# Windowed attention and a softplus feed-forward on one core: q, k and v in rotating buffers, x transposed by DMA from block 6

## The chip, the cores and the metric

The kernel runs on one core of a Trainium2 chip. The metric is the device time of one launch in microseconds. The kernel before takes 225.42 us (median of three runs, 224.99 to 226.09).

## What is computed

Attention over 4 batches, 8 heads, 768 positions and a head size of 64, then a two-layer feed-forward with softplus. Each query sees its own and the 95 positions before it, and the first 8 positions of its batch; a bias falls with the distance, with a slope for each head.

```python
B, H, S, D = 4, 8, 768, 64           # n_global 8, n_local 96
scores = q @ k.T / sqrt(D) - slopes * dist
a = softmax(where(is_global | is_local, scores, -1e9))
x = (a @ v).transpose(0, 2, 1, 3).reshape(3072, 512)
h = x @ w_in                         # w_in 512 x 2048
out = (max(h, 0) + log1p(exp(-abs(h)))) @ w_out   # w_out 2048 x 512, out 3072 x 512
```

All arrays are float32 in memory; the kernel multiplies in bfloat16 and sums in float32.

## The kernel before

The 3072 tokens are cut into 24 blocks of 128 (6 of them a batch) and 12 chunks of 256. Attention goes by blocks, the feed-forward by chunks. The program is a list of named steps, and the order in which they are recorded is the order in which each engine executes its share. The steps for block n:

- `t`: TensorE transposes q and k of the block (4 matmuls each), VectorE copies them to `QT` and `KT`. From block 8 (`NDT`) on it is `d` instead: two transposing DMAs on the SyncE queue (SP), lines 226 and 227.
- `gk`, `gv`: VectorE copies the 8 global rows of the batch's first block into `KT` and `v_t` of the block before.
- `s`: scores of half the heads, 8 matmuls into `s_ps` (line 253), and VectorE adds the bias (`Z`, line 260).
- `e`: ScalarE's exponential (`Pb`, line 266).
- `p`: 8 matmuls of `Pb` with `v_t` into `x_ps` (line 279). A column of ones at the end of each head of `v_t` gives the sum of weights; VectorE divides by it (`xsf`, lines 290 and 293).
- `x`: transposes `xsf` into half of a chunk's `XT`, by TensorE (line 308) and a VectorE copy (line 311) below block 12 (`NDX`), by a transposing DMA on SP from there on (line 304).

The feed-forward has 8 steps `f` a chunk (f0 to f95): 8 matmuls of `w_in` with the chunk's `XT` (line 324), then ScalarE's exponential and logarithm (lines 329, 330). Chunk c reads `XT` of blocks 2c and 2c+1, so f24 to f31 read blocks 6 and 7. It has 8 steps `o` (o0 to o95): 4 matmuls of 512 columns (line 338); after each fourth VectorE copies the sum (`osb`, line 344) and SP stores it (line 346).

`opening()` does blocks 0 and 1 with filler matmuls (`warm`, line 384). Then comes a list written by hand, `ORDER`, up to about f23. All later steps are sorted by due times in units of one `f` (`steady(n)`; `f{u}` at u + 0.5, `o{u}` at u + 13.9).

Loads are issued by GpSimd, cast from float32 to bfloat16 by the DMA: 128 KB as written for each of q, k and v of a block, 512 KB for each quarter of `w_in` and `w_out`. The program before has a buffer of its own for each of the 24 blocks of q, k and v; all loads stand in the GpSimd queue from the start, in the order blocks 1 to 3 with `w_in`, blocks 4 and 5, `w_out`, blocks 6 to 23. A load waits for the landing of the eighth load before it, so at most eight are under way. [...]

Of the kernel before, what the change touches and what calls it, by code (L numbers as in the profile page):

```python
# [12 lines left out]
BF16 = mybir.dt.bfloat16  # L13
# [6 lines left out]
def kernel(  # L20
# [12 lines left out]
    P = nc.NUM_PARTITIONS  # L33

    B, H, S, D = q.shape
# [16 lines left out]
    NWC = 4  # L52
# [7 lines left out]
    const = ctx.enter_context(tc.tile_pool(name="const", bufs=1))  # L60
# [7 lines left out]

    NB = 2 * NCH
    BPB = 2 * CPB  # L70
    q_t = [const.tile([P, H, D], BF16, name=f"q_t{n}") for n in range(NB)]
    k_t = [const.tile([P, H, D], BF16, name=f"k_t{n}") for n in range(NB)]
    v_t = [const.tile([P, H, D + 1], BF16, name=f"v_t{n}") for n in range(NB)]
    w_in_c = [const.tile([P, KM, FW], BF16, name=f"w_in{c}") for c in range(NWC)]
    w_out_c = [const.tile([P, NFB // NWC, DM], BF16, name=f"w_out{c}") for c in range(NWC)]

# [5 lines left out]
    def ones(lo, hi):  # L82
        for n in range(lo, hi):
            nc.vector.memset(v_t[n][:, :, D : D + 1], 1.0)  # L84
# [5 lines left out]
    def load(n, src, dst):  # L90
        b, i = divmod(n, BPB)
        nc.gpsimd.dma_start(  # L92
            dst[n][:, :, 0:D], src[b, :, i * P : (i + 1) * P, :].rearrange("h s d -> s h d")
        )

    def load_w_in(c):
        nc.gpsimd.dma_start(  # L97
            w_in_c[c][:],
            moe_w_in[:, c * FW : (c + 1) * FW].rearrange("(m p) f -> p m f", p=P),
        )  # L100

    def load_w_out(c):
        nc.gpsimd.dma_start(  # L103
            w_out_c[c][:],
            moe_w_out[c * FW : (c + 1) * FW, :].rearrange("(a p) c -> p a c", p=P),
        )

    def load_block(n):
        load(n, q, q_t)
        load(n, k, k_t)  # L110
        load(n, v, v_t)

    _tables = list(get_activation_tables(nc.m.arch).keys())
    nc.scalar.add_instruction(
        mybir.InstLoadActFuncSet(
            name=nc.get_next_instruction_name(),
# [30 lines left out]
    def tables():  # L147
        nc.vector.tensor_scalar(
            far_a[:], rampf[:], float(NL - 1), FAR, op0=ALU.is_gt, op1=ALU.mult
        )  # L150
        nc.vector.tensor_scalar(far_b[:], rampf[:], 0.0, FAR, op0=ALU.is_lt, op1=ALU.mult)
        nc.vector.tensor_tensor(far_a[:], far_a[:], far_b[:], ALU.add)
        nc.vector.tensor_tensor(dist_d[:], far_a[:], rampf[:], ALU.add)
        nc.vector.tensor_copy(dist_0[:], dist_d[:])
        nc.vector.tensor_scalar_min(dist_0[0:NG, :], dist_0[0:NG, :], float(NL))
        nc.vector.tensor_scalar(
            far_b[:], rampf[:], -float(P - NL + 1), FAR, op0=ALU.is_gt, op1=ALU.mult
        )
        nc.vector.scalar_tensor_tensor(dist_p[:], rampf[:], float(P), far_b[:], ALU.add, ALU.add)
        nc.vector.memset(dist_p[0:NG, :], float(NL))  # L160

    tables()
    ones(2, NB)

    load_block(2)
    load_block(3)
    load_w_in(2)
    load_w_in(3)
    load_block(4)
    load_block(5)  # L170
    for c in range(NWC):
        load_w_out(c)
    for n in range(6, NB):
        load_block(n)

    def head_of(half, r):
        return 4 * half + 2 * ((r // 2) % 2) + r // 4
# [1 line left out]
    def bias_first(half):  # L179
        for r in range(0, 8, 2):  # L180
            nc.scalar.mul(bias0[:, half, r // 2, :], dist_0[:], -slopes[head_of(half, r)])

    def bias_rest(half):
        for r in range(8):
            nc.scalar.mul(
                biasA[:, half, r, :], (dist_p if r % 2 else dist_d)[:], -slopes[head_of(half, r)]
            )
# [27 lines left out]
        copy(KT[n][:], tr[:, 1, :, :])  # L215

    NDT = 8
    NDX = 12

    def dma_qk(n):  # L220

# [23 lines left out]
    def sc(n, half):  # L245

        first = n == first_of(n)
        for t in range(1 if first else 2):
            for mm in range(2):
                for sub in range(2):  # L250
                    m = 2 * half + mm
                    rows = slice(64 * sub, 64 * sub + 64)
                    nc.tensor.matmul(  # L253
                        s_ps[:, 4 * sub + 2 * mm + t, :], KT[n - t][rows, m, :], QT[n][rows, m, :]
                    )
        Z = work.tile([P, 8, P], F32, tag="Z", name="Z")
        if first:
            nc.vector.tensor_tensor(Z[:, 0:4, :], s_ps[:, 0:8:2, :], bias0[:, half, :, :], ALU.add)  # L258
        else:
            nc.vector.tensor_tensor(Z[:], s_ps[:], biasA[:, half, :, :], ALU.add)  # L260
        Zt[n, half] = Z

    def ex(n, half):
        nreg = 4 if n == first_of(n) else 8
        Pb = work.tile([P, 8, P], BF16, tag="Pb", name="Pb")
        nc.scalar.activation(  # L266
            Pb[:, 0:nreg, :], Zt.pop((n, half))[:, 0:nreg, :], AF.Exp, scale=inv_sqrt
        )
        Pt[n, half] = Pb
# [28 lines left out]
    def tr_x(n):  # L298
        xsf, _ = xt.pop(n)
        if n % 2 == 0:  # L300
            XT[n // 2] = xtp.tile([P, NPAIR, CT], BF16, tag="XT", name="XT")
        dst = XT[n // 2][:, :, P * (n % 2) : P * (n % 2) + P]
        if n >= NDX:
            nc.sync.dma_start_transpose(dst, xsf[:].rearrange("p h d -> p (h d)"))
            return
        tr = ps.tile([P, 2, NPAIR, P], BF16, tag="tr", name="tr")
        for m in range(NPAIR):
            nc.tensor.transpose(  # L308
                tr[:, 0, m, :], xsf[:, 2 * m : 2 * m + 2, :].rearrange("p a b -> p (a b)"), ident[:]
            )  # L310
        nc.vector.tensor_copy(dst, tr[:, 0, :, :])  # L311
# [20 lines left out]
    def ffn2(c, u):  # L332
# [14 lines left out]


    LAG = 13
    KINDS = {"t": tr_qk, "d": dma_qk, "gk": gk, "gv": gv, "s": sc, "e": ex, "p": pv, "x": tr_x}  # L350

    ORDER = """
        gk2 f0 gv2 t2 f1 s2.0 e2.0 f2 t3 s2.1 e2.1 gk3 f3 p2.0 s3.0 e3.0 f4 p2.1 gv3 s3.1
        e3.1 gk4 f5 x2 p3.0 f6 t4 p3.1 f7 x3 s4.0 f8 f9 s4.1 f10 f11 e4.0 e4.1 t5 o0 o4 gk5 f12
        gv4 p4.0 f13 s5.0 e5.0 o1 p4.1 o2 s5.1 gv5 f14 x4 o3 p5.0 t6 o5 e5.1 p5.1 f15 s6.0 x5 o6
        e6.0 s6.1 e6.1 t7 d8 p6.0 f16 f17 p6.1 s7.0 e7.0 o8 x6 f18 s7.1 gk8 e7.1 d9 o9 p7.0 f19
        f20 p7.1 gv8 s8.0 e8.0 d10 f21 o7 x7 s8.1 e8.1 gk9 f22 p8.0 f23
    """  # L360

    def steady(n):

        s = 4 * n - 13
        return {
            f"d{n}": s - 5.6, f"gk{n}": s - 0.85, f"s{n}.0": s + 0.1, f"e{n}.0": s + 1.2,
            f"s{n}.1": s + 2.1, f"e{n}.1": s + 3.2, f"gv{n}": s + 3.15, f"p{n}.0": s + 3.7,
            f"p{n}.1": s + 5.2, f"x{n}": s + (6.3 if n < NDX else 5.8),
        }

    def run(name):
# [4 lines left out]
        else:  # L376
            KINDS[kind](*nums)

    warm_ps = ps2.tile([P, DM], F32, tag="hT", name="warm_ps")

    def warm(count):

        for _ in range(count):
            nc.tensor.matmul(warm_ps[:], warm_in[:, 0:P], warm_in[:])  # L384

    def tr_first_q(n):
        tr = qk_bank()
        tr_in(tr, 0, q_t[n])
        to_QT(n, tr)

    def tr_first_k(n):
        tr = ps2.tile([P, 2, NPAIR, P], BF16, tag="o", name="tr_k")
        tr_in(tr, 1, k_t[n])
        to_KT(n, tr, nc.vector.tensor_copy if n == 0 else nc.scalar.copy)

    def opening():

        warm(8)
        bias_first(0)
        bias_first(1)  # L400
        bias_rest(0)
        bias_rest(1)
        nc.vector.tensor_copy(q_t[0][:], q_f[:])
        nc.vector.tensor_copy(k_t[0][:], k_f[:])
        tr_first_q(0)
        warm(1)
        tr_first_k(0)
        warm(2)
        sc(0, 0)
        ex(0, 0)  # L410
        tr_first_q(1)
        tr_first_k(1)
        warm(1)
        sc(0, 1)
        ex(0, 1)
        warm(1)
        pv(0, 0)
        sc(1, 0)
        ex(1, 0)
        warm(1)  # L420
        pv(0, 1)
        warm(2)
        sc(1, 1)
        tr_x(0)
        ex(1, 1)
        warm(3)
        pv(1, 0)
        warm(5)
        pv(1, 1)
        warm(3)  # L430
        tr_x(1)
        warm(1)

    opening()
    first_steps = ORDER.split()
    for name in first_steps:
        run(name)
    todo = {}
    for n in range(NDT, NB):
        todo.update(steady(n))  # L440
    for u in range(NU * NCH):
        todo[f"f{u}"] = u + 0.5
        todo[f"o{u}"] = u + LAG + 0.9
# [37 lines left out]
```

## Time and profile before

| | before |
|---|---|
| median of three runs | 225.42 us (224.99 to 226.09) |
| the profiled execution | 224.88 us |
| its span, first to last instruction | 223.1 us |
| granted TensorE clock | 0.997 |
| TensorE busy | 212.8 us (95%) |
| ScalarE busy | 162.6 us (73%) |
| VectorE busy | 116.4 us (52%) |
| GpSimd busy, nearly all in issuing loads | 68.4 us (31%) |
| loads of q, k and v | 70, median 9.4 to 9.5 us from issue to landing |
| transposing DMAs | 44 (16 of q, 16 of k, 12 of x) |

The page of the profile gives busy times of the engines (PE is TensorE, PEld its weight loads, DVE VectorE, ACT ScalarE, POOL GpSimd, SP SyncE), a row of digits for 40 equal slices of the span, the chain of work that ended last, followed back from the end, and the costliest groups of instructions by line. In answers of the trace, the arrow `out<-in` names the tiles written and read, and a bracket gives the engine's idle time before an instruction and what ended it. An engine that is not the bound may sit idle at no cost.

### The profile page before, as it was taken

The page shows a single profiled execution, that of the slowest core. Times are in us where ns is not written, and L with a number is a line of the kernel's source. Part 1 is how long each engine was busy: PE and PEld are TensorE (multiplying, and loading weights), DVE is VectorE, ACT ScalarE, POOL GpSimd, SP SyncE. Part 2 cuts the span into 40 slices and gives each one's busy share as a digit, 9 for nine tenths or more (in the row PEclk, how much of TensorE's full clock was granted, in tenths as well). Part 3 has the DMA queues.
Part 4 walks back from the last instruction along what each step waited for, and adds up shares of the span by engine and source line. Part 5 has one row for each costly group of instructions (what it writes and reads, how often), then busy time and mean ns, then how long its engine had stood idle before and what let it go on. Part 6 is the DMA issues. An engine that isn't in the chain of part 4 may idle for free.

```text
span 223.1 us, 4879 instructions
## 1 busy us (share of the span) xinstructions
PE 212.8 (95%) x1964; PEld 140.2 (63%) x1996; DVE 116.4 (52%) x263; ACT 162.6 (73%) x266; POOL 68.4 (31%) x85
## 2 busy tenths in 40 slices
PE   7889999999899999999999999999999999999993
PEld 2457776677667676667666666666666666666541
DVE  7767864866775565464464563454654653011121
ACT  7738999669698768768878878688788787677200
POOL 8958563696668568550000000000000000000000
PEclk9999999999999999999999999999999999999998
DMA  9999999999999999999912622721433220111112
GB/s 129 164 173 191 167 200 203 158 183 127 150 182 175 156 180 181 130 182 181 156 51 69 119 60 62 121 81 40 118 86 35 72 73 18 53 50 47 47 51 90
DMA packets 106518, 26.27 MB, mean 118 GB/s; under 512 B 99328, under 2 KB 103424, under 8 KB 106496
## 3 DMA queue, kind: packets, MB, share of 16 engines
q0 software_dynamic: 77024, 13.37, 77.4%
q1 hardware_dynamic: 29472, 12.59, 28.3%
q8 instruction: 15, 0.25, 0.4%
q14 instruction: 7, 0.06, 0.1%
HBM read 27.26 MB, written 6.29 MB: 150 GB/s over the span
## 4 chain that ended last, share of the span: by engine, by line
PE 72%; DMA 22%; POOL 3%; issue 1%; DVE 0%; POOLq 0%
PE o L338 33%; PE hT L324 31%; DMA w_in<-in_moe_w_in_dram 9%; DMA w_out<-in_moe_w_out_dram 6%; PE s_ps L253 5%; DMA KT<-k_t 3%; PE x_ps L279 3%; DMA k_t<-in_k_dram 3%; POOL v_t L92 1%; PE tr L308 1%; POOL w_out L103 1%; POOL q_t L92 0%; POOL k_t L92 0%; POOL w_in L97 0%; DVE osb L344 0%
## 5 line engine op out<-in xcount | busy, mean ns | idle before, releaser
L324 PE MATMUL hT<-XT,w_in 128*128 128x256 bf16 x768 | 99.2, 273 | 1.2 <-DVE XT L311 0.7
L338 PE MATMUL o<-w_out,G 128*128 128x512 bf16 x354 | 91.0, 379 | 1.6
L329 ACT ACTIVATE e_sb<-hT 128x512 f32<-128x512 f32 x96 | 56.5, 588 | 35.9 <-PE hT L324 35.7
L324 PEld LDWEIGHTS <-w_in 128*128 128x128 bf16 x768 | 70.6, 98 | 18.2 <-issue 0.7
L330 ACT ACTIVATE G<-e_sb 128x512 bf16<-128x512 f32 x96 | 60.5, 630 | 3.1
L260 DVE TENSOR_TENSOR Z<-s_ps,biasA 128x1024 f32<-128x1024 f32 x40 | 48.8, 1220 | 12.1 <-PE s_ps L253 10.2
L338 PEld LDWEIGHTS <-G 128*128 128x128 bf16 x384 | 36.0, 98 | 27.7
L266 ACT ACTIVATE Pb<-Z 128x1024 bf16<-128x1024 f32 (+1 forms) x48 | 46.6, 973 | 5.4 <-DVE Z L260 4.4
L344 DVE COPY osb<-o 128x512 f32<-128x512 f32 x24 | 16.6, 692 | 44.5 <-PE o L338 44.5
L290 DVE RECIPROCAL rcp<-x_ps 128x4 f32<-128x4 f32 x48 | 8.7, 181 | 37.2 <-PE x_ps L279 37.2
L92 POOL DMA_DIRECT2D v_t<-in_v_dram x24 | 21.3, 888 | 10.8 <-DMA q_t<-in_q_dram 3.9
L92 POOL DMA_DIRECT2D k_t<-in_k_dram x23 | 20.5, 891 | 7.6 <-DMA v_t<-in_v_dram 4.3
L92 POOL DMA_DIRECT2D q_t<-in_q_dram x23 | 20.6, 896 | 4.7 <-DMA k_t<-in_k_dram 2.8
L253 PEld LDWEIGHTS <-KT 64*128 64x128 bf16 x352 | 10.2, 94 | 18.6 <-issue 15.4
L293 DVE TENSOR_TENSOR xsf<-x_ps,rcp 128x256 bf16<-128x256 f32 x48 | 20.4, 424 | 1.7
L279 PEld LDWEIGHTS <-Pb 128*128 128x128 bf16 x352 | 16.8, 98 | 6.6 <-ACT Pb L266 1.1
L253 PE MATMUL s_ps<-QT,KT 64*128 64x128 bf16 x352 | 18.2, 219 | 2.0 <-DMA KT<-k_t 0.9
L279 PE MATMUL x_ps<-v_t,Pb 128*128 128x65 bf16 x352 | 18.6, 193 | 0.4 <-ACT Pb L266 0.3
L384 PE MATMUL warm_ps<-warm_in 128*128 128x512 bf16 x26 | 9.5, 485 | 1.2 <-DVE v_t L84 1.2
L258 DVE TENSOR_TENSOR Z<-s_ps,bias 128x512 f32<-128x512 f32 x8 | 5.5, 690 | 2.8 <-PE s_ps L253 2.6
L243 DVE COPY v_t<-v_t 8x512 bf16<-8x512 bf16 x16 | 5.6, 353 | 0.0
L311 DVE COPY XT<-tr 128x512 bf16<-128x512 bf16 x12 | 5.0, 415 | 0.8 <-PE tr L308 0.8
(39 smaller groups left out, 51.9 us busy)
## 6 DMA issues: line engine op xcount, KB each, us to landing
out_dram<-osb SPq DMA_DIRECT2D x24, 256.0 KB, 2.2
v_t<-in_v_dram POOLq DMA_DIRECT2D x24, 128.0 KB, 9.4
q_t<-in_q_dram POOLq DMA_DIRECT2D x23, 128.0 KB, 9.4
k_t<-in_k_dram POOLq DMA_DIRECT2D x23, 128.0 KB, 9.5
w_in<-in_moe_w_in_dram POOLq DMA_DIRECT2D x4, 512.0 KB, 9.5
w_out<-in_moe_w_out_dram POOLq DMA_DIRECT2D x4, 512.0 KB, 11.8
q_f<-in_q_dram SPq DMA_DIRECT2D x1, 256.0 KB, 3.2
k_f<-in_k_dram SPq DMA_DIRECT2D x1, 256.0 KB, 3.8
```

What stands on the lines that cost most here:

```text
L92: nc.gpsimd.dma_start(dst[n][:, :, 0:D], src[b, :, i * P : (i + 1) * P, :].rearrange("h s d -> s h d"))
L253: nc.tensor.matmul(s_ps[:, 4 * sub + 2 * mm + t, :], KT[n - t][rows, m, :], QT[n][rows, m, :])
L260: nc.vector.tensor_tensor(Z[:], s_ps[:], biasA[:, half, :, :], ALU.add)
L266: nc.scalar.activation(Pb[:, 0:nreg, :], Zt.pop((n, half))[:, 0:nreg, :], AF.Exp, scale=inv_sqrt)
L279: nc.tensor.matmul(x_ps[:, lh, :], Pb[:, r, :], v_t[n - t][:, h, :], start=(t == 0), stop=(t == 1 or first),)
L293: nc.vector.tensor_tensor(xsf[:, h0 : h0 + 4, :], x_ps[:, :, 0:D], rcp[:, h0 : h0 + 4][:, :, None].to_broadcast([P, 4, D]), ALU.mult,)
L324: nc.tensor.matmul(hT[:, j, :], w_in_c[wc][:, m, fo : fo + P], XT[c][:, m, :], start=(m == 0), stop=(m == KM - 1),)
L329: nc.scalar.activation(e_sb[:], hT[:], AF.Exp)
L330: nc.scalar.activation(G[c][:, 2 * u : 2 * u + 2, :], e_sb[:], AF.Ln, bias=1.0)
L338: nc.tensor.matmul(o[:], G[c][:, 4 * kq + a, ns * P : ns * P + P], w_out_c[kq][:, a, :], start=(kq == 0 and a == 0), stop=(kq == NWC - 1 a ...
L344: nc.vector.tensor_copy(osb[:], O.pop((c, ns))[:])
L384: nc.tensor.matmul(warm_ps[:], warm_in[:, 0:P], warm_in[:])
```

## The change

q and k get four buffers each and v eight, shared by the blocks in rotation. The loads of blocks 6 and 7 and later become steps of their own, `l` (q and k) and `lv` (v), in `ORDER` and, from block 8, by due times. A load into a buffer in rotation waits until the block that had it has been read: q and k of block n+4 until q and k of block n are transposed, v of block n+8 until the last reader of v of block n. The column of ones is set eight times instead of 24. `NDX` goes from 12 to 6, so x of blocks 6 to 11 is transposed by DMA on SP. `ORDER` is replaced and reaches f26.

In the new order as built, SP's queue has, between the transposes of blocks 8 and 13: q8, k8, q9, k9, the output of o7, x6, q10, k10, the output of o11, x7, q11, k11, q12, k12, x8, x9.

```diff
-    q_t = [const.tile([P, H, D], BF16, name=f"q_t{n}") for n in range(NB)]
-    k_t = [const.tile([P, H, D], BF16, name=f"k_t{n}") for n in range(NB)]
-    v_t = [const.tile([P, H, D + 1], BF16, name=f"v_t{n}") for n in range(NB)]
+    RQK = 4
+    RV = 8
+    q_r = [const.tile([P, H, D], BF16, name=f"q_t{n}") for n in range(RQK)]
+    k_r = [const.tile([P, H, D], BF16, name=f"k_t{n}") for n in range(RQK)]
+    v_r = [const.tile([P, H, D + 1], BF16, name=f"v_t{n}") for n in range(RV)]
+    q_t = [q_r[n % RQK] for n in range(NB)]
+    k_t = [k_r[n % RQK] for n in range(NB)]
+    v_t = [v_r[n % RV] for n in range(NB)]
...
-    def load_block(n):
+    def load_qk(n):
         load(n, q, q_t)
         load(n, k, k_t)
+
+    def load_v(n):
         load(n, v, v_t)
...
     tables()
-    ones(2, NB)
+    ones(2, RV)
...
-    load_block(4)
-    load_block(5)
-    for c in range(NWC):
-        load_w_out(c)
-    for n in range(6, NB):
-        load_block(n)
...
-    NDX = 12
+    NDX = 6
...
-    KINDS = {"t": tr_qk, "d": dma_qk, "gk": gk, "gv": gv, "s": sc, "e": ex, "p": pv, "x": tr_x}
+    KINDS = {
+        "t": tr_qk, "d": dma_qk, "gk": gk, "gv": gv, "s": sc, "e": ex, "p": pv, "x": tr_x,
+        "l": load_qk, "lv": load_v,
+    }
...
-        gk2 f0 gv2 t2 f1 s2.0 e2.0 f2 t3 s2.1 e2.1 gk3 f3 p2.0 s3.0 e3.0 f4 p2.1 gv3 s3.1
-        e3.1 gk4 f5 x2 p3.0 f6 t4 p3.1 f7 x3 s4.0 f8 f9 s4.1 f10 f11 e4.0 e4.1 t5 o0 o4 gk5 f12
-        gv4 p4.0 f13 s5.0 e5.0 o1 p4.1 o2 s5.1 gv5 f14 x4 o3 p5.0 t6 o5 e5.1 p5.1 f15 s6.0 x5 o6
-        e6.0 s6.1 e6.1 t7 d8 p6.0 f16 f17 p6.1 s7.0 e7.0 o8 x6 f18 s7.1 gk8 e7.1 d9 o9 p7.0 f19
-        f20 p7.1 gv8 s8.0 e8.0 d10 f21 o7 x7 s8.1 e8.1 gk9 f22 p8.0 f23
+        f0 t2 l6 lv6 gk2 gv2 f1 s2.0 e2.0 f2 t3 l7 lv7 s2.1 gk3 e2.1 f3 p2.0 s3.0 e3.0 f4 p2.1
+        gv3 s3.1 e3.1 gk4 f5 x2 p3.0 f6 t4 l8 p3.1 f7 gv4 x3 s4.0 f8 f9 e4.0 s4.1 f10 e4.1 t5 l9
+        f11 gk5 o0 f12 s5.0 p4.0 o4 e5.0 f13 o1 p4.1 gv5 lv8 s5.1 e5.1 o5 o2 p5.0 x4 f14 p5.1 t6
+        l10 o3 f15 lv9 s6.0 x5 e6.0 o6 s6.1 e6.1 t7 l11 d8 p6.0 f16 f17 d9 s7.0 e7.0 p6.1 o7 f18
+        s7.1 o8 o9 e7.1 p7.0 o10 x6 gk8 d10 f19 lv10 p7.1 gv8 f20 l12 s8.0 e8.0 f21 o11 s8.1 o12
+        gk9 p8.0 e8.1 f22 lv11 s9.0 f23 p8.1 e9.0 x7 o13 gv9 s9.1 o14 e9.1 f24 l13 gk10 p9.0 f25
+        s10.0 f26 lv12 d11 d12 p9.1
...
-            f"p{n}.1": s + 5.2, f"x{n}": s + (6.3 if n < NDX else 5.8),
+            f"p{n}.1": s + 5.2, f"x{n}": s + 5.8,
...
     opening()
+    load_block(4)
+    load_block(5)
+    for c in range(NWC):
+        load_w_out(c)
...
+    for n in range(RV, NB):
+        todo[f"l{n}"] = 4 * n - 27
+        todo[f"lv{n}"] = 4 * n - 21.5
```

More of the change, by code (lines that the diff above doesn't have):

```diff
@@ L106, in load_w_out, with load_block @@
         )
-    def load_block(n):
+    def load_qk(n):
         load(n, q, q_t)
         load(n, k, k_t)
+    def load_v(n):
         load(n, v, v_t)
+    def load_block(n):
+        load_qk(n)
+        load_v(n)
     _tables = list(get_activation_tables(nc.m.arch).keys())
```

## The prediction

> **What bounds the kernel now.** I read the page first, then the chain of waits, then the timeline of TensorE (PE), then the landing times of the transposing DMAs in two stretches. From the page, busy time, the DMA row of the 40 slices, and the chain's shares:
>
> ```profile
> PE 212.8 (95%) x1964; PEld 140.2 (63%) x1996; DVE 116.4 (52%) x263; ACT 162.6 (73%) x266; POOL 68.4 (31%) x85
> ...
> DMA  9999999999999999999912622721433220111112
> ...
> PE 72%; DMA 22%; POOL 3%; issue 1%; DVE 0%; POOLq 0%
> ```
>
> PE sets the time; the 22% of DMA in the chain lies early, and the DMA engines are full for the first 20 slices (to about 108 us) and nearly empty later. Where DMA enters the chain last:
>
> ```profile
> 41.85 7.24 DMA k_t<-in_k_dram
> 49.11 7.60 DMA KT<-k_t
> 56.76 0.40 PE s_ps L253 x8
> ```
>
> k of block 8 lands, is transposed by DMA in 7.6 us, and PE waits for it. In the table of PE's waits none is later than this one. The timeline of PE around it (start, duration, idle before in brackets):
>
> ```profile
> 53.69 1.91 PE L324 MATMUL hT<-XT,w_in 128*128 128x256 bf16 x16
> 55.43 0.41 PE L279 MATMUL x_ps<-v_t,Pb 128*128 128x65 bf16 x8
> 56.76 0.40 PE L253 MATMUL s_ps<-QT,KT 64*128 64x128 bf16 x8 [0.92 <-DMA KT<-k_t]
> ...
> 62.78 0.41 PE L279 MATMUL x_ps<-v_t,Pb 128*128 128x65 bf16 x8
> 63.03 1.04 PE L324 MATMUL hT<-XT,w_in 128*128 128x256 bf16 x8
> 63.90 1.03 PE L338 MATMUL o<-w_out,G 128*128 128x512 bf16 x4
> 64.86 0.40 PE L253 MATMUL s_ps<-QT,KT 64*128 64x128 bf16 x8
> 65.19 0.40 PE L308 MATMUL tr<-ident,xsf 128*128 128x128 bf16 x4
> 65.42 1.04 PE L324 MATMUL hT<-XT,w_in 128*128 128x256 bf16 x8
> 66.30 1.03 PE L338 MATMUL o<-w_out,G 128*128 128x512 bf16 x4
> 67.16 1.04 PE L324 MATMUL hT<-XT,w_in 128*128 128x256 bf16 x8
> ```
>
> Matmuls overlap, so a step's price is the distance of starts: f 0.87 (63.03 to 63.90), o 0.86 (66.30 to 67.16), s 0.33 (64.86 to 65.19), p 0.25 (62.78 to 63.03), a PE transposition of x 0.23 (65.19 to 65.42). Last, the DMA transposes of k, from issue to landing, first while loads fill the queues (57 to 106 us), then after them (106 us on):
>
> ```profile
> L227 SPq DMA_TRANSPOSE KT<-k_t x6: 1282/1344/1675, 56.6 to 101.2; - x6
> DMA to landing us min/median/max: 7.0/7.6/8.2
> ...
> L227 SPq DMA_TRANSPOSE KT<-k_t x8: 1195/1216/1220, 109.4 to 167.1; - x8
> DMA to landing us min/median/max: 2.4/2.4/3.9
> ```
>
> The same transfer takes 2.4 us alone and 7.6 us beside the loads. This pair of rows decides the case.
>
> **The change, part by part.** *x by DMA from block 6.* x6 to x11 leave PE: 6 x 0.23 = 1.4 us, all on the path, as PE is the bound where they stand (51 to 91 us). Their 6 VectorE copies (0.42 us each) were beside PE's work: nothing. *Memsets.* Sixteen fewer of the v ones (17 take 0.64 us in VectorE's timeline): nothing, because the cast of k behind them sits idle 0.46 us for its own DMA. *Loads.* Their number and prices stay (0.88 us of GpSimd each). Each now also waits until its rotating buffer is read; behind a waiting load stand only later loads. Load n is due 4n-27, its DMA transpose 4n-18.6: 8.4 steps of f, and a block of four takes 8.3 us (starts 105.0 to 113.3 us), so 17 us, against 9.5 us that a load takes in full queues. Nothing. Up to k of block 8 the sequence of loads is what it was, so 49.1 us stays the landing of k8 and about 56.7 us that of its transpose.
>
> *The order.* Ahead of f20 now stand two more o steps (o7, o10) and p7.1, and no x6: 0.86 + 0.86 + 0.25 - 0.23 = 1.7 us. So f20, at 54.56 before (0.87 behind the row of 53.69), starts at 56.3, and the scores of block 8 behind it at 57.1, after their KT has landed: the 0.92 us of waiting is covered. If that transpose took 8.2 us, 0.2 us of it would come back.
>
> *The new wait.* f24 needs x7 transposed. On PE it was made at 58.8 and f24 started at 63.0 without a wait. Now x7 is a DMA on SP, behind the output of o11, which waits for VectorE's copy of o11. PE reaches the end of o11 after f20, s8.0, f21, o11: 56.3 + 0.87 + 0.33 + 0.87 + 0.86 = 59.2, 0.2 more until its results are out; copy 0.69 (osb group of the page), output issue 0.33 and pauses 0.2: x7 is issued at about 60.6. PE is ready for f24 after s8.1, o12, p8.0, f22, s9.0, f23, p8.1, o13, s9.1, o14 more: 3 x 0.33 + 3 x 0.86 + 2 x 0.25 + 2 x 0.87 = 5.8, so at 59.2 + 5.8 = 65.0. x7 has 4.4 us. The landing is bounded by the rows above: 2.4 us (no wait) and 8.2 us (wait 3.8); 8.5 is the longest for q (3.9 ... 4.1). Which is nearer? By 60.6 us the load sequence has run as before through v of block 10; q12 and k12 then wait for the transposes of q8 and k8 (about 55 and 57 us) and v11, q13, k13 follow at GpSimd's 0.9 us, so some five loads stand in the queues where before there were eight, but SP has three transposes and two outputs of its own in flight. I take 7.2 us, a little under the median of the full queues: x7 lands at 67.8, f24 waits 2.8 us. Nothing hides this: f24 to f31 all read that x, and what stands behind f24 on PE is p9 and more f.
>
> [...]
>
> *Later DMA transposes.* x9 for f32 and x11 for f40 have 7.4 us (x13 was issued at 105.85, f48 started at 113.3): enough for anything up to 7.4, short by 0.8 at worst each; loads are 3 per 8.3 us by then, so I take nothing. After the wait the f steps stand close, with ScalarE at 0.59 + 0.63 us each, but ScalarE has emptied its queue during the wait: nothing.
>
> **Sum.** -1.4 (x on PE) - 0.9 (KT of block 8) + 2.8 (x7) = +0.5 us. The profiled execution took 224.88 us for a span of 223.1 (1.8 lie around it, unchanged), so 225.4; that execution lay 0.5 below the median of 225.42, so the median becomes 225.9.
>
> **Rivals.**
>
> *1. x7 lands in time.* [...] Time: 225.42 - 1.4 - 0.9 = 223.1. For it: five loads instead of eight, and the idle-queue rows. Against: every transpose of q and k issued from 47 to 100 us took 7.0 or more.
>
> *2. x7 lands much later, and PE cools.* SP's transposes stand closer than before: K9, x6, Q10, K10 and two outputs ahead of x7. If two of these are served first at 1.3 us each on top of 7.2, x7 takes 9.8 us, lands at 70.4 and f24 waits 5.4. Then PE may restart slowly, as at the kernel's start:
>
> ```profile
> 1.19 3.60 PE L384 MATMUL warm_ps<-warm_in 128*128 128x512 bf16 x8 [1.19 <-DVE v_t L84]
> ...
> 12.57 1.24 PE L384 MATMUL warm_ps<-warm_in 128*128 128x512 bf16 x5
> ```
>
> Eight matmuls start 0.42 us apart there ((3.60 - 0.63)/7, where 0.63 is the longest one), five later 0.21 apart ((1.24 - 0.38)/4): half speed for the first 3 us or so costs 1.7. The granted clock reads 1.00 in both stretches, so the row of granted clock doesn't show this. Time: 225.42 - 2.3 + 5.4 + 1.7 = 230.2; without the slow restart 228.5. It is slower than now from a wait of 3.4 us on. [...]
>
> *3. A load comes late for its transpose,* which takes a landing of over 17 us from issue where the profile has 9.5: little speaks for it. Each missed block would cost what the transpose is late; 2 us once gives 227.8.
>
> **How the numbers follow.** About 0.5%, 1.1 us, is what a measurement of this kernel can tell from no change. The net is zero at a wait of 2.3 us, so the wait at f24 is the sign: under 1.2 faster, over 3.4 slower. Forecast case (wait 1.2 to 3.8 us, 224.3 to 226.9): 0.47, of which 0.07 lie over the bound. Rival 1, with waits below 1.2 us (223.1 to 224.3): 0.25. Rival 2, with waits over 3.8 us (226.9 to 230.2): 0.24. Rival 3: 0.04. So faster 0.25, same 0.40, slower 0.07 + 0.24 + 0.04 = 0.35. The range takes in all of rival 1 (0.2 more at its low end for the spread of the runs) and the lower third of rival 2: 222.9 to 228.0.
>
> **What would show it.** Right: no wait for KT at the scores of block 8, no PE transposition of x behind block 5, PE idle for 2 to 4 us before f24 near 65 us with the DMA of XT as its end, the same 8.3 us a block behind 100 us. Wrong: XT landing under 5 us from issue near 61 us (rival 1), an idle time of 4 us or f steps over 1.5 us apart behind it (rival 2), or PE waiting for q_t, k_t or v_t (rival 3).

## The result and the profile after

The changed kernel takes 228.51 us (median of four runs, 227.82 to 229.32) against 225.75 us for the kernel before (four runs, 224.99 to 227.04): a ratio of 1.013, interval 1.0089 to 1.0172. It is slower by 2.8 us. Medians in this document are over all runs, and ratios leave out runs over 1.5% above the fastest of the same kernel: two of the kernel with x7 issued earlier (226.47 and 226.57 us) and one of that with x of blocks 6 and 7 by TensorE (274.98 us, at a granted clock of 0.758). The forecast was 225.9 us, and its range ended at 228.0. The profiled execution of after took 228.09 us for a span of 226.3, which is 3.2 us over the profiled execution of before.

From the page of after, the busy time of TensorE (PE), the rows of the granted clock and of the DMA engines in 40 slices, and the chain's shares:

```profile
PE 212.5 (94%) x1941; PEld 139.1 (61%) x1972; DVE 113.2 (50%) x241; ACT 162.9 (72%) x266; POOL 68.3 (30%) x85
...
PEclk9999999999996999999999999999999999999999
DMA  9999999999999915999799969993622220211112
...
PE 81%; DMA 8%; POOL 4%; ACT 3%; DVE 2%; issue 1%; SPq 0%; POOLq 0%
```

PE executes 23 instructions fewer and yet is busy for almost the same time. One slice of the clock, the 13th (67.9 to 73.5 us), reads 6. DMA's share of the chain fell from 22% to 8%: k of block 8 no longer stands in it. What stands in it now is this (the chain of waits of after, start and duration):

```profile
59.42 0.70 DVE osb L349
...
60.14 0.33 SPq L351
...
60.52 8.70 DMA XT<-xsf
69.22 0.14 issue
69.36 1.26 PE hT L329 x8
```

The copy of o11, its output, x of block 7 behind it on SP, 8.70 us until that has landed, then f24. The timeline of PE in the same place (idle before in brackets):

```profile
57.14 0.40 PE L258 MATMUL s_ps<-QT,KT 64*128 64x128 bf16 x8
...
64.47 1.04 PE L343 MATMUL o<-w_out,G 128*128 128x512 bf16 x4
69.36 1.26 PE L329 MATMUL hT<-XT,w_in 128*128 128x256 bf16 x8 [3.85 <-DMA XT<-xsf]
70.41 0.65 PE L284 MATMUL x_ps<-v_t,Pb 128*128 128x65 bf16 x8
...
74.20 0.41 PE L284 MATMUL x_ps<-v_t,Pb 128*128 128x65 bf16 x8
```

The scores of block 8 (57.14) have no bracket: that wait is gone. PE is ready for f24 at 65.33 (64.47 and 0.86 for an o step) and starts it at 69.36, 4.03 us later. The step f24 is 1.05 us long (69.36 to 70.41), where an f step takes 0.87. Stretches of this execution, with the granted clock in the column PEclk:

```profile
core 0: us, PE busy (x) PEld busy (x) DVE busy (x) ACT busy (x) POOL busy (x), PEclk, DMA share, GB/s
63.20:66.61 3.41, 2.26 (x20) 0.81 (x17) 2.40 (x6) 3.04 (x5) 2.45 (x3) 1.00 1.86 198
66.61:70.03 3.42, 0.68 (x7) 0.64 (x8) 0.00 (x0) 0.36 (x1) 0.17 (x1) 1.00 1.69 127
70.03:73.44 3.41, 3.41 (x30) 2.25 (x28) 0.63 (x3) 1.84 (x4) 1.75 (x2) 0.50 1.96 153
73.44:76.85 3.41, 3.36 (x35) 2.79 (x34) 1.81 (x3) 3.00 (x6) 0.00 (x0) 1.00 1.82 155
```

The clock changes at 70.03 and 73.44 us; the other bounds lie 3.41 us from one to the next. PE was idle for most of 66.61 to 70.03, and in the next 3.41 us, when it had work again, its clock was 0.50.

The account of the profiled execution: -1.4 (x of blocks 6 to 11 off PE), -0.9 (no wait for KT of block 8), +4.03 (f24's wait), +1.5 (half clock; the price is worked out below): +3.2 us. The starts of f16 and f40 in the two traces moved apart by 3.22 us. From f40 on, every f start sampled keeps that distance, so nothing behind it matters.

### The profile page after: what moved, and what is told of

It reads as the page before. It is cut to its first block, busy times and chain, and to the rows that moved or that the text cites. A ratio compares the mean times of both kernels' runs of the same rounds, so it can differ in the third digit from the quotient of the medians.

```text
span 226.3 us, 4863 instructions
## 1 busy us (share of the span) xinstructions
PE 212.5 (94%) x1941; PEld 139.1 (61%) x1972; DVE 113.2 (50%) x241; ACT 162.9 (72%) x266; POOL 68.3 (30%) x85
## 4 chain that ended last, share of the span: by engine, by line
PE 81%; DMA 8%; POOL 4%; ACT 3%; DVE 2%; issue 1%; SPq 0%; POOLq 0%
PE hT L329 36%; PE o L343 35%; PE s_ps L258 5%; DMA k_t<-in_k_dram 4%; PE x_ps L284 4%; DMA XT<-xsf 4%; ACT Pb L271 1%; POOL q_t L97 1%; POOL v_t L97 1%; PE tr L208 1%; POOL k_t L97 1%; POOL w_in L102 1%; ACT e_sb L334 1%; DVE osb L349 1%; ACT G L335 1%
## 5 line engine op out<-in xcount | busy, mean ns | idle before, releaser
L329 PE MATMUL hT<-XT,w_in 128*128 128x256 bf16 x768 | 100.6, 275 | 5.0 <-DMA XT<-xsf 3.8
L394 PE MATMUL warm_ps<-warm_in 128*128 128x512 bf16 x26 | 8.9, 459 | 1.2 <-DVE v_t L89 1.2
L394 PEld LDWEIGHTS <-warm_in 128*128 128x128 bf16 x28 | 2.8, 112 | 3.6 <-issue 1.7
L248 DVE COPY v_t<-v_t 8x512 bf16<-8x512 bf16 x16 | 4.8, 300 | 0.0
```

The costliest lines, as they stand in the source:

```text
L329: nc.tensor.matmul(hT[:, j, :], w_in_c[wc][:, m, fo : fo + P], XT[c][:, m, :], start=(m == 0), stop=(m == KM - 1),)
```

## Experiments

The theory from the two traces (A in the expectations): the loss is the wait of f24 for x of block 7 and the slow restart behind it, and the rest of the change gains. Four questions follow: is it this one transfer, why does it take 8.7 us, is the restart real and what brings it on, and what does each half of the change do alone? The kernel before took 225.1 us (median of 25 runs), 225.06 (21), 225.16 (17) and 224.97 (5) beside the four groups of runs.

### Is it x of block 7?

**x7 issued earlier.** x7 goes right behind p7.1, ahead of the transposes of q and k of block 10.

```diff
-        ... x6 gk8 d10 f19 lv10 p7.1 gv8 f20 l12 ... p8.1 e9.0 x7 o13 gv9 ...
+        ... x6 gk8 f19 lv10 p7.1 x7 d10 gv8 f20 l12 ... p8.1 e9.0 o13 gv9 ...
```

> The changed kernel with two steps moved: x7 is recorded right behind p7.1, and d10 (the DMA transposes of q and k of block 10) behind x7, so that on SP x7 stands ahead of q10, k10 and the output of o11. x7 should be issued near 57 us instead of 60.5. If its landing takes 8 to 8.7 us whatever stands before it on SP (theory: the DMA queues are full of loads), it lands at 65 to 66 us, f24 waits 0 to 0.7 us, k10 lands near 68 us and the scores of block 10 may wait up to 1 us: 223.1 to 224.3 us. If the wait at f24 were not the cause (theory B), the time stays above 225.7 us.

Measured: 223.58 us, ratio 0.9929 (0.9902 to 0.9956). x7 is issued at 56.88 and lands at 63.97. From its timeline:

```profile
65.26 1.04 PE L329 MATMUL hT<-XT,w_in 128*128 128x256 bf16 x8
...
68.24 0.40 PE L258 MATMUL s_ps<-QT,KT 64*128 64x128 bf16 x8 [0.83 <-DMA KT<-k_t]
```

f24 starts at 65.26 without a wait. What was moved back pays: KT of block 10 now comes 0.83 us late. Two steps in another place (x7, and d10 behind it) turn the change from 2.8 us slower to 1.5 us faster.

**x of blocks 6 and 7 by TensorE** (`NDX = 8` in after).

> The changed kernel with x of blocks 6 and 7 transposed by TensorE again (NDX 8). Theory A (the loss is the wait at f24, 4.0 us, and a slow restart behind it, about 1.4 us; the rest of the change gains about 2.3 us): no wait at f24, TensorE pays 2 x 0.23 us, and the time is 228.5 - 5.4 + 0.5 = 223.6 us, some 1% under the kernel before. Theory B (rotation and order cost something elsewhere, the wait at f24 only takes up slack that another wait would take): the time stays above 225.7 us and another wait of over 1 us shows on TensorE.

Measured: 223.81 us, ratio 0.993 (0.9905 to 0.9955).

**x of block 7 alone by TensorE.**

```diff
-        if n >= NDX:
+        if n >= NDX and n != 7:
```

> The changed kernel with x of block 7 alone by TensorE; block 6 and 8 onward by DMA. Theory A: no wait at f24, none for k of block 10, 0.23 us of TensorE: 0.2 to 0.6 us under the two kernels that kept f24 from waiting (223.8 and 223.6), 223.0 to 223.6 us and some 0.8% under the kernel before. Otherwise, if blocks 8 to 11 by DMA bring waits of their own, 224 us or more.

Measured: 223.81 us, ratio 0.9931 (0.9901 to 0.9962), 0.2 over what was expected. Its timeline shows part of what was missed:

```profile
79.91 1.03 PE L329 MATMUL hT<-XT,w_in 128*128 128x256 bf16 x8 [0.46 <-DMA XT<-xsf]
```

Without the stall at f24 everything behind comes 4 us earlier, and x of block 9, 8.83 us from issue to landing, is then the next to be late, for f32. All three kernels take back the loss, so it is this transfer and what hangs on it.

### Why 8.7 us?

Two theories: SP's own transposes just ahead of x7 delay it, or the loads in the queues do.

**q and k of block 10 by TensorE** (`t10` in place of `d10`), so that two of SP's transposes ahead of x7 go.

> The changed kernel with q and k of block 10 transposed by TensorE instead of two DMAs on SP: two transposes less stand on SP ahead of x7, the loads are the same but for the one into block 10's buffers. Theory C (the landing of x7 is set by SP's own DMAs ahead of it): its 8.7 us falls by 2 x 1.2 to 1.3 us, to about 6.2. Theory D (it is set by the loads in the queues): it stays at 7.5 to 9 us.

One run: 226.76 us. x7 still takes 8.05 us (61.22 to 69.27).

**Six loads fewer.** The loads of q and k of blocks 12 and 13 and of v of blocks 11 and 12 are left out; those blocks compute with what their buffers held before.

> The changed kernel without six loads that stand in the queues when x7 is issued: q and k of blocks 12 and 13, v of blocks 11 and 12 are left out, and those blocks compute with what an earlier block left in the buffers. SP's own DMAs ahead of x7 are the same. Theory D (loads set the landing): x7 lands 3 to 5 us from issue instead of 8.7, f24 waits 0 to 0.5 us and the time is about 223 to 223.5 us. Theory C (SP's own queue): it still takes 7 us or more and f24 waits over 2 us.

One run: 224.12 us, 0.6 over the expectation. The issue and landing of x7 (tile `XT`, window 60 to 63 us):

```profile
L309 SPq DMA_TRANSPOSE XT<-xsf x1: 1284/1284/1284, 61.3 to 61.3; - x1
DMA to landing us min/median/max: 4.6/4.6/4.6
```

It lands in time and f24 doesn't wait. In after six loads were under way when x7 was issued (the last of them just being issued), here one; SP's own DMAs were all there. So the loads make some 4 of the 8.7 us. What SP's own DMAs make is less: 0.65 us came off without the transposes of block 10 (single runs both, and x7 took 8.79 to 8.98 us in the kernels with fillers below, which issue the same DMAs as after), and with x7 first, where neither these two nor the output of o11 stand ahead of it, it still took 7.09 (56.88 to 63.97).

The packets in the traces show where the time goes (q0 are the loads, q1 is SP's queue; the numbers are packets, MB and a share of the engines' time, over 100% where packets overlap). In after from 64 to 65 us, where q1 has no row, and from 66 to 69.2 us:

```profile
q0 software_dynamic: 1224, 0.15, 242.6%
...
q1 hardware_dynamic: 1025, 0.28, 91.9%
q0 software_dynamic: 1025, 0.13, 75.4%
```

The output of o11 and x7 behind it were issued at 60.14 and 60.52, and yet from 64 to 65 us no packet of SP's ran. From 65 to 66 us q1 had 118 packets with 0.23 MB, by their size of 2 KB the output's. From 66 us up to the landing of x7 the two queues had as many packets each. With q and k of block 10 off SP, q1 had none from 62.5 to 64.5 us: with less work ahead on SP, the gap was longer. With the six loads left out, q0 had none from 62.5 to 63.5 us and q1 had 504. So over half of the 8.7 us (60.52 to about 66) passes before x7's packets begin, if SP's DMAs run in the order of issue. Why SP's packets come so late while loads run is not shown, nor what the 2.2 us are by which 4.64 lies over the 2.4 of idle queues.

### The slow restart

**Fillers ahead of f24.** n matmuls of 512 columns that nobody reads, in front of f24, keep PE at work for part of the wait or all of it. They write a PSUM buffer of f24's kind, and do not move x7.

```diff
-        ... s9.1 o14 e9.1 f24 ...
+        ... s9.1 o14 e9.1 w18 f24 ...
...
+    def fill(count):
+        ps_f = ps2.tile([P, DM], F32, tag="hT", name="fill_ps")
+        for _ in range(count):
+            nc.tensor.matmul(ps_f[:], warm_in[:, 0:P], warm_in[:])
```

> The changed kernel with 18 filler matmuls of 512 columns (18 x 0.215 = 3.9 us) right before f24; the result is not used. x7 lands when it did, so f24 starts near 69.4 us as before. Theory A with a clock that falls while TensorE idles: behind the filler f24 to f26 keep 0.87 us of eight matmuls and the granted clock stays full, so 1.4 us come back: 227.1 us. Rival (the slow steps behind f24 come from ScalarE or the operands, not from the idle time): the steps stay at 1.0 to 1.8 us and the time at 228.5 us.

With 18: 227.08 us, ratio 1.0087 (1.0052 to 1.0122), 1.4 us under after although PE does more and x7 lands later (69.89). Taken by the ratios, each to the runs of before beside it, it is 1.0 us (1.0130 less 1.0087), and the two intervals overlap: the medians alone don't show the gain. The traces and the clocks do. From its timeline:

```profile
65.88 4.05 PE L399 MATMUL fill_ps<-warm_in 128*128 128x512 bf16 x18
70.02 1.03 PE L329 MATMUL hT<-XT,w_in 128*128 128x256 bf16 x8
...
73.31 0.41 PE L284 MATMUL x_ps<-v_t,Pb 128*128 128x65 bf16 x8
```

From f24 to the second p step behind it: 3.29 us here (70.02 to 73.31), 4.84 in after (69.36 to 74.20). The restart costs 1.5 us in these two traces. In all ten runs the mean granted clock was 0.996 or more; in after it was 0.992 in two runs (227.82 and 228.09 us) and 0.985 in two (228.94 and 229.32). One stretch of 3.41 us at half clock takes 0.0075 off the mean of 226 us, so by this estimate these are one such stretch and two.

How much idle time does it take? The kernel with block 10 by TensorE had waited for 3.19 us and had restarted at full clock, so the first guess was a length between 3.2 and 3.85 us. Three more counts of fillers tested it.

> The kernel after with 5 filler matmuls (5 x 0.215 = 1.1 us) ahead of f24, which adds work but leaves the wait for x7's landing where it was; the wait is cut from 4.0 to about 2.5-2.9 us. Theory A (the clock falls only when the idle time is long enough: 3.2 us of it did not do so, 3.85 us did): f24 starts when x7 lands, near 69.4-69.9 us, the granted clock behind it is 1.00, and the time is that of the kernel with 18 fillers, 227.1 us. Theory B (any stall behind which f24 stands costs the restart, and the 18 fillers helped because they left none): granted clock near 0.67 behind f24 and 228.4 us.

> 3 filler matmuls (0.65 us) ahead of f24: the idle time before f24 is about 3.2-3.5 us. If the point from which PE restarts slowly lies between the 3.19 us that left the clock alone and the 3.85 us that did not, the runs fall on both sides: most lose the 1.5 us (228.4 us, mean granted clock 0.992), some do not (227.0 us, clock 1.00). If only the length of the idle time counts and its point is under 3 us, all runs lose it.

> 9 filler matmuls (1.9 us) ahead of f24: the idle time before f24 is about 2.0 us and x7 lands when it did. No run restarts slowly: mean granted clock 0.996 or more in every run, 227.1 us as with 18 fillers. If runs with a clock of 0.992 or less appear here too, as in three of the four runs with 5 fillers, the length of the idle time is not what decides.

| fillers | idle before f24, profiled execution | its mean clock | median of all runs, ratio (interval) | runs at clock 0.992 or less |
|---|---|---|---|---|
| 18 | none | 1.000 | 227.08, 1.0087 (1.0052 to 1.0122) | 0 of 10 |
| 9 | 2.04 us | 1.000 | 228.15, 1.0146 (1.0085 to 1.0206) | 2 of 3 |
| 5 | 2.88 us | 1.000 | 227.91, 1.0119 (1.0067 to 1.017) | 3 of 4 |
| 3 | 3.29 us | 1.000 | 227.77, 1.0134 (1.0076 to 1.0192) | 2 of 3 |
| 0 (after) | 3.85 us | 0.992 | 228.51, 1.0130 (1.0089 to 1.0172) | 4 of 4 (two of them 0.985) |

The expectation for 9 fillers fell: two of its three runs lost the clock with an idle time of about 2 us, if x7 landed in them as in the profiled one. So the length alone doesn't decide. The traces show the granted clock and the work of PE ahead of it. In after the clock was full up to 70.03 us, half for 3.41 us and full from 73.44 us on; in the 3.42 us ahead of the half clock PE was at work for 0.68 us, as the rows above have it. The kernel before ends in the same way, with 0.82 us of work in the 3.41 us ahead:

```profile
218.46:221.87 3.41, 0.82 (x4) 0.20 (x2) 0.69 (x1) 0.00 (x0) 0.00 (x0) 1.00 0.20 77
221.87:223.10 1.23, 0.00 (x0) 0.00 (x0) 0.00 (x0) 0.00 (x0) 0.00 (x0) 0.50 0.00 0
```

With block 10 by TensorE, two stretches of this length that hold the wait of 3.19 us between them, and the one behind:

```profile
64.09:67.50 3.41, 2.12 (x16) 0.73 (x14) 2.55 (x6) 3.02 (x5) 1.27 (x2) 1.00 1.85 188
67.50:70.92 3.42, 1.52 (x20) 1.42 (x21) 0.18 (x1) 0.63 (x2) 0.00 (x0) 1.00 1.76 146
70.92:74.33 3.41, 3.41 (x43) 2.84 (x42) 2.18 (x4) 3.29 (x7) 1.76 (x2) 1.00 1.80 154
```

The clock stays at 1.00. So little work in 3.41 us doesn't decide alone either: a stretch cut around this wait would hold 0.22 us of work (3.41 less 3.19), under the 0.68 of after. What decides besides is not shown, and the runs of 9 fillers that lost the clock were not traced.

### One part of the change alone

**The rotating buffers and the new order, with x by TensorE as before** (`NDX = 12` in after).

> The changed kernel with x of blocks 6 to 11 by TensorE as in the kernel before (NDX 12): rotating buffers, paced loads and the new order alone. Theory A: what is left is the gain at the transpose of block 8, 0.9 us less than before: 224.2 us beside 225.1. Rival (the 0.9 us gap comes back elsewhere, or the order costs): 225 us or more.

Measured: 223.87 us, ratio 0.9945 (0.9919 to 0.9972). Between f16 and f40 it gains 0.99 us on before: the wait for KT of block 8, and nothing else. So the rotating loads cost nothing that shows there.

**x by DMA from block 6 in the kernel before** (`NDX = 6` there, all else as it was).

> The kernel before with x by DMA from block 6 on (NDX 6): all loads at once, the old order. Theory D: x7 stands behind the output of o7 on SP, is issued near 60 us and lands at 67.5 to 68.5 us; f24 is ready near 62.6, waits about 5 us and restarts slowly; later transposes of x also take 7 to 8 us while the loads last, with 0 to 1 us more at f32 and f40: 225.1 - 1.4 + 5.2 + 1.4 + 0.5 = 230.8 us. If the wait of the changed kernel came from the rotation (loads that wait for transposes), there is no such wait here and it takes 223.7 us.

Measured: 233.5 us, ratio 1.0357 (1.03 to 1.0413), 2.7 us over the expectation. From its chain and its stretches:

```profile
60.52 9.09 DMA XT<-xsf
```

```profile
64.58:67.99 3.41, 0.00 (x0) 0.00 (x0) 0.41 (x1) 0.97 (x2) 0.87 (x1) 1.00 1.87 200
67.99:71.40 3.41, 1.74 (x8) 1.25 (x10) 0.00 (x0) 0.00 (x0) 1.59 (x2) 0.50 2.01 107
71.40:74.82 3.42, 3.20 (x18) 1.52 (x18) 1.53 (x2) 1.23 (x2) 3.04 (x5) 0.50 2.25 154
```

With all loads queued from the start, eight at a time, x7 takes 9.09 us and f24 waits for 5.35. The clock is at half for 6.83 us (67.99 to 74.82), where after had 3.41: the first of the two stretches has the end of the stall in it, and PE works in 1.74 of its 3.41 us. That, and waits of 1.42 and 0.91 us for KT where before had one of 0.92, is most of what the expectation lacked.

### A better version

**x7 first, and q and k of block 10 by TensorE,** to take away the 0.83 us that was left.

> x7 issued right behind p7.1, and q and k of block 10 transposed by TensorE instead of SP's DMAs. Against the kernel with x7 first alone (223.6 us): the wait of 0.83 us for KT of block 10 goes, 8 transposes of 0.055 us each, 0.45 us, are added: 223.2 us, if nothing else is late. Rival: the next wait behind it (for q, k of a later block, or x of a later one) takes its place, 223.6-224.0 us.

Measured: 223.56 us, ratio 0.9935 (0.9908 to 0.9963), the same as x7 first alone (223.58). The rival is what its trace shows: the wait for KT is gone, and f32 waits for x of block 9 instead (the two transposes of x issued from 68 to 71 us took 8.5 us or more).

```profile
79.65 1.05 PE L329 MATMUL hT<-XT,w_in 128*128 128x256 bf16 x8 [0.26 <-DMA XT<-xsf]
```

With the 0.45 us of transposes added, 0.1 of the 0.83 us is left, less than the runs can tell.

The versions without the stall can't be told apart: 223.56 to 223.87 us, ratios from 0.9929 to 0.9945 with intervals that overlap. Among them is the one with x of blocks 6 to 11 all by TensorE (223.87). So the rotation and the new order beat the kernel before by 0.6%, and that x by DMA adds to it is not shown: the 1.4 us that it takes off PE goes in part into other waits (0.83 us with x7 first). x7 first, at 0.7% under before, is no safe choice either: two of its ten runs took 226.47 us (at a clock of 0.992) and 226.57, and what was late in them was not traced.

## Why the prediction was wrong

- **x off PE, -1.4: right in after.** From f28 to f40 the starts of after come 0.67 us nearer to those of before, three transpositions of 0.22.
- **KT of block 8, -0.9: right.** f20 starts at 56.17 (56.3 said), the scores at 57.14 without a wait; 0.99 us with x left on PE.
- **Loads: nothing. Right.** No load of q, k or v ended a wait of PE behind 20 us in after.
- **Issue of x7 at 60.6 and f24 ready at 65.0: right**, 60.52 and 65.33.
- **The landing of x7, 7.2 us: the step that failed.** It took 8.70, so the wait was 4.03 us and not 2.8, 1.2 us of the miss. The argument was that five loads instead of eight would bring it "a little under the median of the full queues". There were six, and the transpose was nearly as slow behind six loads as behind eight: 8.70 and 9.09. What it left out is the time before x7's packets begin, over 4 us in after. The bound from above was 8.2 us, the longest of the rows for k between 56 and 101 us, so even the far end of the wait, 3.8, was too short; the 8.5 us of q, named beside it, was nearer.
- **No slow restart in the forecast case: the other failed step,** 1.5 us of the miss. It was priced rightly in rival 2 (1.7 us by the kernel's opening matmuls, 1.5 measured) but tied to a wait of 5.4 us. At 4 us every run of after showed a half clock in its mean, and in the kernels with 3 to 9 fillers, whose traces have 2 to 3.3 us of idle time, 7 of 10 did. With it, the forecast's own middle, a wait of 2.8 us, would have cost up to 4.3 (2.8 + 1.5).
- **The rivals.** Rival 2 is what happened, by its own mark (a wait over 3.8 us, a slow restart) and by its time (226.9 to 230.2). Its chance of 0.24 and a range cut at its lower third were too small, for the longest row of k alone, 8.2 us, puts the wait at its limit of 3.8. Its cause, two transposes served ahead of x7, is not the one: taking away two transposes left 8.05 us. Rival 1's landing under 5 us came only when loads were left out (4.64). Rival 3 did not show.
- **x9 and x11 in time: right in after, where the stall moved all behind it.** With the stall gone, x9 took 8.83 us against the 7.4 reckoned and cost 0.46.
- **Together:** +0.5 forecast, +1.2 from the wait, +1.5 from the clock: +3.2, against 3.2 us between the profiled executions and 2.8 between the medians.

## What to carry to other kernels

A step moved from a compute engine to a DMA must be issued a full landing time ahead of its reader, and that time is read from the same kind of transfer in the same stretch, at its longest: here 8.7 to 9.1 us beside the loads, 2.4 us on idle queues. Its place in the issuing queue sets when it is issued (60.52 behind the output of o11, 56.88 ahead of it), so put the transfer with the nearest reader first. A stall of TensorE may cost a slow restart besides: 11 of the 14 runs of after and of the kernels with 3, 5 and 9 fillers, whose traces have stalls of 2.04 to 3.85 us, had a mean clock of 0.992 or less, and in after's trace 3.41 us at half clock cost 1.5 us. And ask what the step gains once its waits are gone: here the kernel with all of x on TensorE was as fast.

## What the runs showed that was not expected

The kernels with 3, 5 and 9 fillers, which have stalls of 2.04 to 3.29 us in their traces, lost the clock in 7 of their 10 runs and kept it in 3: with 5 fillers it took 226.78 us at a clock of 1.000 and 227.75 to 228.93 at 0.992. In the 3.4 us ahead of a half clock PE was at work for 0.68 us (after) and 0.82 us (the end of the kernel before); with x by DMA in the kernel before, the half clock went on for another 3.42 us behind a stretch with 1.74 us of work. And with 18 matmuls that nobody reads the mean clock was 0.996 or more in all ten runs, and the median came down with it, by 1.0 to 1.4 us, within the spread of the intervals.
